# Decode attention plus MLP on one core: inner loops with computed addresses, w2 in 13 rows, and the selects moved to the end of a unit

## The chip, the cores and the metric

The kernel runs on one core of one Trainium2 chip. Time is what the device needs for one execution, in microseconds (us): the median of several runs. A profiled execution of its own gives the rows that are quoted; its clock starts with the span. The engines are TensorE (PE, with its weight loads as PEld), VectorE (DVE), ScalarE (ACT), GpSimd (POOL) and SyncE (SP), which here issues nearly all DMAs into one queue.

## The reference, cut to what matters

```python
x = A_x                                  # (8, 1, 640), bf16
xn = _layernorm(x)
return x + A(xn, k_cache, v_cache, wq, wo) + B(xn, w1, b1, w2, b2)

# A: decode attention, B=8, 32 heads, 4096 keys, Dh=128, one query each
q = (x @ wq).reshape(B, 1, 32, 128).transpose(0, 2, 1, 3)
scores = einsum("bhqd,bhkd->bhqk", q, k_cache) * 128 ** -0.5
o = einsum("bhqk,bhkd->bhqd", softmax(scores), v_cache)
return o.transpose(0, 2, 1, 3).reshape(B, 1, 4096) @ wo

# B: y = layernorm(x); gelu(y @ w1 + b1) @ w2 + b2, F = 1728
```

The two caches are 268 MB each and are read once. Everything else is about 15 MB.

## The kernel before, in words

The work is cut into 32 **units**. Unit i is one batch row and one group of 8 heads: K(i) and V(i), 8.39 MB each, every one loaded by a single DMA of 128 descriptors of 64 KB. A partition holds 256 keys of one head (16 partitions to a head). K(i) goes to slot KA or KB by turns, V(i) to the one slot VS. SyncE's queue holds the order K0, K1, V0, K2, V1, K3, V2 and so on; `load_k(i)` waits until slot i-2 is free, `load_v(i)` until the product P times V of unit i-1 is done (`pv`), and what stands behind a waiting load waits too.

Scores of a unit are made in two ways at once. For 176 of the 256 keys of a partition, VectorE multiplies K by the broadcast query and sums over Dh (`dve_chunk`: a product, a sum of the two halves, a reduction), in three chunks of 58, 59 and 59 keys. For the other 80 keys TensorE transposes K (`pe_T`, ten tiles of 8 keys), ScalarE copies each tile from PSUM (`act_T`, an eviction), and TensorE multiplies it by the query (`pe_QK`). That yields 8 candidates for each key, of which a mask picks one: the **selects** (`dve_sel`, a product and a reduction in PSUM, twice 40 keys), between the second chunk and the third. `dve_max` finds the maximum and makes the bias of the softmax; `act_exp` runs eight exponentials on ScalarE; `pe_RS` sums them; `pe_PV` multiplies by V in 256 matmuls; `act_O`, `dve_rinv` and `o_norm` scale the result.

The query's broadcast for VectorE is a matmul (`pe_qbc`) and an eviction (`act_qbc`); before, both run ahead of K's arrival. A tiny memset on GpSimd (`k_ready`) waits for K(i), and TensorE waits for that memset.

The order of each engine is written by hand: every step has a position (`at(o + 52, dve_sel, i, 0)`), the steps are recorded in that order for each engine, and then replayed into instruction streams. Part of the units is recorded as loops: on VectorE and ScalarE 15 turns of two units after two unrolled units, on TensorE a loop over all units after the first. In a TensorE turn stand the broadcast and scores of unit r, then row sum and P times V of unit r-1. On ScalarE the exponentials of unit i stand after the evictions of unit i+1 for i = 0 alone; later ones stand ahead of them (position 90):

```python
at(o + 52, dve_sel, i, 0)
at(o + 55, dve_sel, i, 1)
at(o + 58, dve_chunk, i, 2)
at(o + 84, dve_max, i)
at(o + 90 if i else o + Q + 45, act_exp, i)
at(o + Q + 48, pe_RS, i)
at(o + Q + 57, dve_rinv, i)
at(o + Q + 50, pe_PV, i)
```

Ahead of the units: layer norms, q = xn @ wq (160 matmuls, after wq has landed), and the MLP. Its first layer needs w1's columns spread out, by ten copies on VectorE and ScalarE (`spread_w1`); its second layer has w2 in 128 half rows of 13.5 rows each, with zeros beside them and 136 matmuls (`pe_mlp2`). K1 and V0 wait for q's last matmul (`qw`), since their slots hold weights until then. Behind the units: wo, in part through selection matmuls and folds (`pe_sel`, `dve_fold`, `fin_wl`, `fin_wn`), and the store.

Of the kernel before, what the change touches and what calls it, by code (L numbers as in the profile page):

```python
# [14 lines left out]
P = 128  # L15
# [12 lines left out]
class _Eng:  # L28
# [17 lines left out]
    def sig(self, inst):  # L46
        self.n += 1
        inst.call[3] = (self.sem, 1)
        return (self.sem, self.n)

# [17 lines left out]
class _Slot:  # L68


    def __init__(self, slots, i, lo, n):
        self.slots, self.i, self.lo, self.n = slots, i, lo, n

    def at(self, i):
        return self.slots[:, i % 2, self.lo:self.lo + self.n]
# [29 lines left out]
def _emit(e, call, wait=None, turn=None):  # L105
    name, a, k, inc = call
    a = [x.at(x.i if turn is None else turn) if isinstance(x, _Slot) else x for x in a]
    if name == "wait_ge":
        e.wait_ge(a[0], a[1] if wait is None else wait, **k)
        return  # L110
    inst = getattr(e, name)(*a, **k)  # L111
    if inc is not None:
        inst.then_inc(*inc)


def _replay(e, calls):
    for call in calls:
        _emit(e, call)


def _same(x):
    if isinstance(x, _Slot):
        return ("slot", x.lo, x.n)
    if hasattr(x, "ap") and hasattr(x, "offset"):
        return (x.tensor.name, x.offset, str(x.ap), str(x.dtype))
    return str(x)


def _steps(turns):

    body = turns[0]
    assert len({len(t) for t in turns}) == 1, [len(t) for t in turns]
    grow = []
    for j, (name, args, kw, inc) in enumerate(body):
        step = 0
        for r in range(1, len(turns)):
            name_r, args_r, kw_r, inc_r = turns[r][j]
            assert name_r == name and inc_r == inc and sorted(kw_r) == sorted(kw), (j, name, name_r)
            if name == "wait_ge":
                assert args_r[0] is args[0]  # L140
                if r == 1:
                    step = args_r[1] - args[1]
                assert args_r[1] == args[1] + r * step and args[1] > 0 and step >= 0, (j, args, args_r)
            else:
                assert [_same(x) for x in args_r] == [_same(x) for x in args], (j, name)
                assert [_same(kw_r[x]) for x in sorted(kw)] == [_same(kw[x]) for x in sorted(kw)], (j, name)
        grow.append(step)
    return grow


def _replay_loop(e, calls, a, b, n):

    size = (b - a) // n
    assert size * n == b - a and n >= 2
    _replay(e, calls[:a])
    grow = _steps([calls[a + r * size:a + (r + 1) * size] for r in range(n)])
    with e.bass.Fori(0, n, engines=OrderedEngineSet([e.engine])) as r:
        for call, step in zip(calls[a:a + size], grow):
            _emit(e, call, call[1][1] + r * step if step else None)
    _replay(e, calls[b:])  # L160


def _replay_pe(e, calls, head, mid, end, late):
# [4 lines left out]
    g1, g2 = _steps(first[:-1]), _steps([[c for c in t if not _late(c, late)] for t in second])  # L168
    _replay(e, calls[:head[0]])
    with e.bass.Fori(1, n + 1, engines=OrderedEngineSet([e.engine])) as r:  # L170
        reg = e.to_reg(r)
        with e.If_lt(reg, n):
            for call, step in zip(first[0], g1):
                _emit(e, call, call[1][1] + (r - 1) * step if step else None, r)
        g = iter(g2)
        for call in second[0]:
            if _late(call, late):
                e.wait_ge(call[1][0], (r >> (n.bit_length() - 1)) * 16 + 1)
            else:
                step = next(g)  # L180
                _emit(e, call, call[1][1] + (r - 1) * step if step else None)
        with e.If_eq(reg, n - 1):
            _replay(e, first[-1])
    assert n & (n - 1) == 0
    _replay(e, calls[end:])


def _late(call, late):
    return call[0] == "wait_ge" and any(call[1][0] is x for x in late)


def bass_parallel_sum__gqa_block_cached__mixer_channel_mlp__decode_kernel(
# [23 lines left out]
    FQ = F // (P // 2)  # L216
    FH = FQ // 2
    PAD = D // 10
    SCALE = float(DH) ** -0.5
    TPB = 8  # L220
    NS = 2
    LOOP0, LOOPN = 2, 15
# [6 lines left out]
    assert FQ * (P // 2) == F and FQ == 2 * FH + 1  # L229

    def jp_of(i):
        return 80

    def chunks(i):
        jd = NKEY - jp_of(i)
        n = 3
        return [(jd * c // n, jd * (c + 1) // n) for c in range(n)]
# [3 lines left out]

    group0 = [0]
    for i_ in range(NQ):
        group0.append(group0[-1] + jp_of(i_) // TPB)
# [4 lines left out]
    with ExitStack() as es:  # L249
# [4 lines left out]
        S_sb = sb("S_sb", [P, 3, SLOT], BF)  # L254
        tile = [S_sb[:, s, :].rearrange("p (j d) -> p j d", d=DH) for s in range(3)]
# [16 lines left out]

        w2_sb = scratch(F * D // P + 2 * PAD)
        b1_sb = scratch(F, 1).rearrange("p (c f) -> p c f", c=1)
        b1r_sb = scratch((FH + 1) * P, 1).rearrange("p (c j m) -> p c j m", c=1, m=P)
        w1r_sb = scratch(DC * (FH + 1) * P).rearrange("p (c j m) -> p c j m", c=DC, m=P)
# [6 lines left out]
        hT_sb = scratch((FH + 1) * B).rearrange("p (c b) -> p c b", b=B)  # L283
        hh_sb = scratch(2 * (FH + 1) * B).rearrange("p (w c b) -> p w c b", w=2, b=B)
        par_sb = scratch(4).bitcast(F32)
        iota_i = scratch(2 * P).bitcast(I32)
        iota_h = scratch(2 * HS).bitcast(I32)
        mtmp = scratch(2 * 2 * HS).bitcast(F32).rearrange("p (w n) -> p w n", w=2)
        ones_sb = scratch(B, 1)
        zeros_sb = scratch(P)  # L290
        assert o_[0] <= SLOT

        KT_sb = sb("KT_sb", [P, NS, TPB, P], BF)
        Sd_sb = sb("Sd_sb", [P, 2, NKEY], F32)
# [6 lines left out]
        oU_sb = sb("oU_sb", [P, 2, HS], F32)  # L301
# [3 lines left out]
        mx_sb = sb("mx_sb", [P, 32], F32)  # L305
        mxT_sb = sb("mxT_sb", [P, 32], F32)
        mq_sb = sb("mq_sb", [P, 2], F32)
        mb_sb = sb("mb_sb", [P, 32], F32)
        mbT_sb = sb("mbT_sb", [P, 32], F32)
        NB_sb = sb("NB_sb", [P, 2, HS], F32)  # L310
# [3 lines left out]
        kr_sb = sb("kr_sb", [P, 1], F32)  # L314
# [8 lines left out]
        ACC_ps = ps("ACC_ps", [P, 512], F32)  # L323
        TRB, SBK = [_Bank(), _Bank()], [_Bank(), _Bank()]
        PVB, QBB, CHB, ACCB = _Bank(), _Bank(), _Bank(), _Bank()
        QT_ps = CH_ps[:, 0:H * B]
        HT_ps = CH_ps[:, H * B:H * B + (FH + 1) * B]
        RS_ps = CH_ps[:, 384:384 + HS]
        OUT_ps = QB_ps[:, :].bitcast(BF)
        assert H * B + (FH + 1) * B <= 384  # L330
# [21 lines left out]

        def load_k(i):
            s = kslot(i)
            if i >= 2:
                sp.wait(tk[("kt", i - 2)], tk[("km", i - 2)])
            elif s == KB:
                sp.wait(tk["qw"])
            tk[("k", i)] = ld_s[s].sig(sp.dma_start(tile[s], cache_src(A_k_cache, i)))

# [13 lines left out]
        def load_wl(q):  # L374
            sp.wait(tk[("kt", NQ - 2)], tk[("km", NQ - 2)])
# [12 lines left out]
        def consts_pool():  # L388
            pool.iota(iota_h, [[-HP, HS]], base=0, channel_multiplier=1)
            tk["iota"] = pool.sig(pool.iota(iota_i, [[1, P]], base=0, channel_multiplier=-1))  # L390
            for d, (ap, v) in zip([None] * (6 - len(ld_vl)) + ld_vl, (
                    (zeros_sb, 0.0), (w2_sb[:, 0:PAD], 0.0), (w2_sb[:, PAD + F * D // P:], 0.0), (ones_sb, 1.0),
                    (mx_sb[:, :], 0.0), (mb_sb[:, :], 0.0))):
# [487 lines left out]
```

## Time and profile before

| | |
|---|---|
| Median of 3 runs | 1283.71 us (1283.64 to 1284.03) |
| Profiled execution | 1283.58 us, its span 1282.3 us |
| Bytes read | 551.80 MB, 430 GB/s over the span |
| Busy: PE, DVE, ACT, POOL | 667.4 (52%), 1099.9 (86%), 483.8 (38%), 98.6 us (8%) |
| Mean granted TensorE clock | 0.592 |

A row of the chain has start, length, and what ran or what was waited for. A row of the timeline has start, length, engine, operation, output and inputs, a count, and in brackets how long the engine had been idle and what ended that. SPq and ACTq are issues of DMAs. All helper lines are L111, so groups are told by their tiles.

### The profile page before, as it was taken

The page shows a single profiled execution, that of the slowest core. Times are in us where ns is not written, and L with a number is a line of the kernel's source. Part 1 is how long each engine was busy: PE and PEld are TensorE (multiplying, and loading weights), DVE is VectorE, ACT ScalarE, POOL GpSimd, SP SyncE. Part 2 cuts the span into 40 slices and gives each one's busy share as a digit, 9 for nine tenths or more (in the row PEclk, how much of TensorE's full clock was granted, in tenths as well). Part 3 has the DMA queues.
Part 4 walks back from the last instruction along what each step waited for, and adds up shares of the span by engine and source line. Part 5 has one row for each costly group of instructions (what it writes and reads, how often), then busy time and mean ns, then how long its engine had stood idle before and what let it go on. Part 6 is the DMA issues. An engine that isn't in the chain of part 4 may idle for free.

```text
span 1282.3 us, 34538 instructions
## 1 busy us (share of the span) xinstructions
PE 667.4 (52%) x13994; PEld 569.3 (44%) x13994; DVE 1099.9 (86%) x677; ACT 483.8 (38%) x908; POOL 98.6 (8%) x112
## 2 busy tenths in 40 slices
PE   4463555564544664544654544654545655545645
PEld 3352444453443553433553534543434544434545
DVE  3599998988888988888988888988889988889885
ACT  3343333344432344423344423344323444323441
POOL 1011110000000000000000000000000000000001
PEclk9955565565656666556666556665556655556655
DMA  9999999999999999999999999999999999999998
GB/s 401 449 421 434 433 431 431 438 433 431 431 440 431 431 431 440 431 429 433 442 429 429 433 442 429 431 431 442 431 430 431 444 427 433 429 444 427 433 419 358
DMA packets 11509, 552.00 MB, mean 430 GB/s; under 512 B 1245, under 2 KB 2278, under 8 KB 2279
## 3 DMA queue, kind: packets, MB, share of 16 engines
q1 hardware_dynamic: 11424, 551.79, 99.6%
q8 instruction: 9, 0.15, 0.0%
q10 hardware_dynamic: 70, 0.03, 0.0%
q14 instruction: 6, 0.04, 0.0%
HBM read 551.80 MB, written 0.01 MB: 430 GB/s over the span
## 4 chain that ended last, share of the span: by engine, by line
DMA 74%; PE 17%; DVE 7%; issue 1%; ACT 0%; SPq 0%; DVEq 0%; ACTq 0%
DMA S_sb<-in_A_v_cache_dram 69%; PE PV_ps L111 16%; DVE S_sb L111 4%; DMA S_sb<-in_A_k_cache_dram 3%; DVE Sd_sb L111 2%; DMA S_sb<-in_A_wo_dram 2%; PE TR_ps L111 1%; ACT P_sb L111 0%; PE S_ps L111 0%; DVE S_ps L111 0%; SPq L111 0%; ACT KT_sb L111 0%; DVE mx_sb L111 0%; PE ACC_ps L111 0%; DVE mxT_sb L111 0%
## 5 line engine op out<-in xcount | busy, mean ns | idle before, releaser
L111 PE MATMUL TR_ps<-ident_bf,S_sb 128*128 128x128 bf16 (+1 forms) x2570 | 340.6, 270 | 363.5 <-POOL kr_sb L111 344.8
L111 DVE TENSOR_TENSOR S_sb<-S_sb,qbc_sb 128x7552 bf16<-128x7552 bf16 (+1 forms) x96 | 388.7, 4049 | 124.7 <-DMA S_sb<-in_A_k_cache_dram 124.3
L111 PEld LDWEIGHTS TR_ps<-ident_bf,S_sb 128*128 (+2 forms) x2570 | 243.4, 102 | 423.7 <-issue 351.6
L111 DVE TENSOR_REDUCE Sd_sb<-S_sb 128x59 f32<-128x3776 bf16 (+1 forms) x96 | 390.2, 4064 | 6.0
L111 ACT ACTIVATE KT_sb<-TR_ps 128x1024 bf16<-128x1024 bf16 x320 | 327.1, 1024 | 116.6 <-PE TR_ps L111 106.8
L111 PE MATMUL PV_ps<-P_sb,S_sb 128*128 128x8 bf16 x8192 | 224.3, 175 | 144.5 <-DMA S_sb<-in_A_v_cache_dram 140.5
L111 PEld LDWEIGHTS PV_ps<-P_sb,S_sb 128*128 128x128 bf16 x8192 | 221.3, 103 | 147.4 <-DMA S_sb<-in_A_v_cache_dram 143.2
L111 ACT ACTIVATE P_sb<-Sd_sb,NB_sb 128x256 bf16<-128x256 f32 x256 | 126.3, 494 | 229.0 <-DVE NB_sb L111 229.0
L111 DVE TENSOR_TENSOR S_sb<-S_sb 128x3776 bf16<-128x3776 bf16 (+1 forms) x96 | 202.9, 2114 | 3.3
L111 ACT ACTIVATE oU_sb<-PV_ps 128x8 f32<-128x8 f32 x31 | 5.5, 178 | 384.3 <-PE PV_ps L111 384.3
L111 PE MATMUL S_ps<-qrep_sb,KT_sb 128*128 128x8 bf16 x2560 | 121.3, 177 | 51.7 <-ACT KT_sb L111 48.5
L111 PEld LDWEIGHTS S_ps<-qrep_sb,KT_sb 128*128 128x128 bf16 x2560 | 90.7, 101 | 82.1 <-ACT KT_sb L111 35.9
L111 POOL TENSOR_TENSOR oT_sb<-oU_sb,ri_sb 128x8 bf16<-128x8 f32 x31 | 69.3, 2235 | 383.5 <-DVE S_sb L111 341.8
L111 POOL COPY qrep_sb<-qT_sb 128x128 bf16<-128x128 bf16 x32 | 19.7, 615 | 477.6 <-PE S_ps L111 451.4
L111 ACT ACTIVATION_READ_ACCUMULATOR P_sb<-Sd_sb,NB_sb 128x1 f32 x256 | 47.8, 187 | 0.0
L111 DVE TENSOR_REDUCE Sd_sb<-S_ps 128x40 f32<-128x320 f32 x64 | 31.4, 491 | 2.2
L111 DVE TENSOR_TENSOR S_ps<-S_ps,mask_sb 128x320 f32<-128x320 f32 (+1 forms) x66 | 32.7, 495 | 0.0
L111 POOL MEMSET kr_sb<- 128x1 f32 x32 | 3.1, 98 | 293.4 <-DMA S_sb<-in_A_k_cache_dram 293.4
L111 ACT ACTIVATE qbc_sb<-QB_ps 128x128 bf16<-128x128 f32 x32 | 8.9, 278 | 41.8 <-PE QB_ps L111 41.8
L111 PE MATMUL QB_ps<-ident_bf,qrep_sb 128*128 128x128 bf16 x32 | 9.1, 284 | 26.1 <-DVE S_sb L111 15.0
L111 PE MATMUL CH_ps<-rs_sb,ones_f 128*128 128x8 f32 x64 | 15.4, 313 | 4.6 <-ACT P_sb L111 4.2
L111 PEld LDWEIGHTS QB_ps<-ident_bf,qrep_sb 128*128 128x128 bf16 x32 | 3.3, 104 | 29.0 <-ACT oU_sb L111 21.0
(58 smaller groups left out, 142.4 us busy)
## 6 DMA issues: line engine op xcount, KB each, us to landing
S_sb<-in_A_wq_dram SPq DMA_DIRECT2D x1, 5120.0 KB, 25.4
S_sb<-in_B_w_dram SPq DMA_DIRECT2D x2, 2160.0 KB, 11.1
S_sb<-in_A_v_cache_dram SPq DMA_DIRECT2D x1, 4096.0 KB, 15.3
S_sb<-in_A_v_cache_dram SPq DMA_DIRECT2D x1, 2816.0 KB, 18.6
S_sb<-in_A_wo_dram SPq DMA_DIRECT2D x1, 2560.0 KB, 31.2
S_sb<-in_A_wo_dram SPq DMA_DIRECT2D x1, 1280.0 KB, 33.9
S_sb<-in_A_v_cache_dram SPq DMA_DIRECT2D x1, 1280.0 KB, 21.4
S_sb<-in_A_wo_dram SPq DMA_DIRECT2D x1, 640.0 KB, 22.6
```

What stands on the lines that cost most here:

```text
L111: inst = getattr(e, name)(*a, **k)
```

## The change

1. **VectorE's chunks** become one of 176 keys. The two selects move behind it (positions 80 and 82), with 64 and 16 keys. The score, bias and unscaled output buffers are single instead of double, so the reduction of unit i waits for the exponentials of unit i-1.
2. **K's arrival** is waited for by the broadcast matmul `pe_qbc`, ahead of transposes and of VectorE's product; GpSimd's marker goes. `pe_qbc` also waits for both PSUM banks of scores, that is for the selects of the unit before. `act_qbc` of unit i+1 stays ahead of the exponentials of unit i on ScalarE.
3. **K's slot** is free with the last select (`s`), where it was with the last reduction and transpose.
4. **Inner loops**: ScalarE's ten evictions are five turns of two, with computed waits; TensorE's scores of unit 0 and 13 columns of the first layer are loops with computed addresses. Loops over units start earlier (VectorE at unit 0, ScalarE at unit 2, one unit a turn).
5. **MLP**: w1 is read with a stride instead of being spread; the last 64 columns are doubled on GpSimd. w2 comes as 13 rows to a partition and 64 single rows to every other partition, over zeros; 70 matmuls instead of 136. The 64 rows and b2 are issued on SyncE, behind a wait for the memset of the zeros.
6. The exponential that loaded ScalarE's table early (`act_O(-1)`) is a copy; two layer norm steps are merged; two folds at the end are one.

```diff
         def load_k(i):
             s = kslot(i)
             if i >= 2:
-                sp.wait(tk[("kt", i - 2)], tk[("km", i - 2)])
+                sp.wait(tk[("s", i - 2)])
...
+        def load_w2():
+            tk["w2"] = [ld_w2.sig(sp.dma_start(
+                w2_sb[:, 0:FR * D], B_w2[0:FR * P].rearrange("(p r) n -> p (r n)", r=FR)))]
+            sp.wait((ld_s[KB].sem, 1))
+            tk["w2"] = [ld_w2.sig(sp.dma_start(w2_sb[0:P:2, FR * D:], B_w2[FR * P:]))]
...
         def pe_qbc(i):
-            pe.wait(tk[("qrep", i)], tk["id"])
+            pe.wait(tk[("qrep", i)], *tk[("kk", i)])
             QBB.use(pe)
+            for b_ in SBK:
+                b_.use(pe)
...
+        def scores(i):
+            n = jp_of(i) // TPB
+            last = None
+            for u in range(n // 2):
+                act.calls.append(["_in", (u,), {}, None])
+                if i == 0:
+                    pe.calls.append(["_in", (u,), {}, None])
+                for t in (2 * u, 2 * u + 1):
+                    pe_T(i, t)
+                    act_T(i, t)
+                    if i == 0 and t % 2:
+                        pe_QK(i, t - 1)
+                        pe_QK(i, t)
+                    elif i and t:
+                        pe_QK(i, t - 1)
...
         def dve_chunk(i, c):
-            dve.wait(tk[("k", i)], tk[("qb", i)])
+            dve.wait(tk[("qb", i)])
...
-            dve.wait(t, tk.get(("exp", i - 2)))
+            dve.wait(t, tk[("exp", i - 1)])
...
         def act_O(i):
             PVB.use(act)
+            act.wait(tk.get(("on", i - 1)), tk[("ri", i)])
...
-            at(o - 2, k_ready, i)
             at(o - 11, pe_qbc, i)
             at(o - 10.5, act_qbc, i)
...
+            at(o, scores, i)
             at(o + 2, dve_chunk, i, 0)
-            at(o + 26, dve_chunk, i, 1)
-            at(o + 52, dve_sel, i, 0)
-            at(o + 55, dve_sel, i, 1)
-            at(o + 58, dve_chunk, i, 2)
+            at(o + 80, dve_sel, i, 0)
+            at(o + 82, dve_sel, i, 1)
             at(o + 84, dve_max, i)
             at(o + 90 if i else o + Q + 45, act_exp, i)
```

523 lines of the change are left out of this document (284 added, 239 removed).

## The prediction

> **What bounds the kernel now.** I read the page first (span, the 40 slices, the shares of the chain), then the chain of waits in order of time, and then the timeline of each engine for the first 145 us. K(i), V(i) are the two 8.39 MB loads of unit i.
>
> ```profile
> span 1282.3 us, 34538 instructions
> DMA  9999999999999999999999999999999999999998
> GB/s 401 449 421 434 433 431 431 438 433 431 431 440 431 431 431 440 431 429 433 442 429 429 433 442 429 431 431 442 431 430 431 444 427 433 429 444 427 433 419 358
> q8 instruction: 9, 0.15, 0.0%
> DMA 74%; PE 17%; DVE 7%; issue 1%; ACT 0%; SPq 0%; DVEq 0%; ACTq 0%
> 434.87 7.01 PE PV_ps L111 x256
> 441.90 31.63 DMA S_sb<-in_A_v_cache_dram
> 473.57 7.01 PE PV_ps L111 x256
> 1279.33 0.72 PE ACC_ps L111 x20
> ```
>
> The transfers never stop: every slice but the last is 90% busy or more. The chain alternates 31.6 us of a V load and 7.0 us of P times V, 38.70 us per unit (434.87 to 473.57), that is 19.35 us per load. PE's 17% costs nothing: while it runs, the next K load flows. So only three things can move the time: bytes, the two ends, or a moment in which the single load queue has nothing left. In steady state it is well filled:
>
> ```profile
> 415.60 4.02 DVE L111 TENSOR_TENSOR S_sb<-S_sb,qbc_sb 128x7424 bf16<-128x7424 bf16 x1 [4.29 <-DMA S_sb<-in_A_k_cache_dram]
> 449.81 0.23 DVE L111 TENSOR_SCALAR NB_sb<-off_sb,mbT_sb 128x8 f32<-128x8 f32 x1
> 454.29 4.02 DVE L111 TENSOR_TENSOR S_sb<-S_sb,qbc_sb 128x7424 bf16<-128x7424 bf16 x1 [4.26 <-DMA S_sb<-in_A_k_cache_dram]
> ```
>
> A K load has landed at 454.29; V is issued at 441.90, 12.4 us before it would be missed, and DVE has 4.3 us to spare in each unit. The start is tighter, because DVE works off a backlog there:
>
> ```profile
> 79.08 0.33 SPq L111 DMA_DIRECT2D S_sb<-in_A_k_cache_dram  x1
> 96.64 0.33 SPq L111 DMA_DIRECT2D S_sb<-in_A_v_cache_dram  x1
> 46.33 0.10 POOL L111 MEMSET kr_sb<- 128x1 f32 x1 [9.41 <-DMA S_sb<-in_A_k_cache_dram]
> 144.58 0.10 POOL L111 MEMSET kr_sb<- 128x1 f32 x1 [3.03 <-DMA S_sb<-in_A_k_cache_dram]
> 0.74 0.39 SPq L111
> 9.57 8.39 ACT L111 ACTIVATE S_sb<-S_sb 128x896 bf16<-128x896 bf16 x5 [2.59 <-DMA S_sb<-in_B_w_dram]
> 1280.96 0.30 ACTq L111 DMA_DIRECT2D out_dram<-out_sb  x1
> ```
>
> K(0) landed at 46.3 and K(3) at 144.55 (GpSimd's memsets wait for them). The order is K0 K1 V0 K2 V1 K3, so V(1) landed near 144.55 - 19.35 = 125.2. How late may V(1) be issued? A load into an empty queue costs its bytes plus an overhead: w1 was issued first, at 0.74, and landed at 9.57 for 2.21 MB, 5.1 us at the steady 433 GB/s (8.39 MB in 19.35 us): 3.7 us over. That was a cold start. I take 2.5 us, midway between this and the 1.3 us from the output's issue (10 KB, 1280.96) to the end of the span. V(1) is then late from 125.2 - 19.35 - 2.5 = **103.35** on; before, it was issued at 96.64, 6.7 us early.
>
> **The change part by part: unit 0 and 1.** V(1) waits for PV(0), PV(0) for exp(0), and ScalarE has exp(0) behind all evictions of unit 1, in both kernels. Before, the transposes of unit 1 began when K(1) landed, 66.40, and were done when exp(0)'s bias came. Now the query's broadcast matmul of unit 1 waits for both selects of unit 0 (it uses the banks' tickets), the transposes of unit 1 stand behind it on TensorE, and the selects are the last work of unit 0 on VectorE. So evictions, exp(0) and PV(0) follow VectorE instead of running beside it. Durations:
>
> ```profile
> 36.97 0.29 PE L111 MATMUL QB_ps<-ident_bf,qrep_sb 128*128 128x128 bf16 x1 [0.87 <-POOL qrep_sb L111]
> 37.29 0.28 ACT L111 ACTIVATE qbc_sb<-QB_ps 128x128 bf16<-128x128 f32 x1 [14.13 <-PE QB_ps L111]
> 46.30 4.02 DVE L111 TENSOR_TENSOR S_sb<-S_sb,qbc_sb 128x7424 bf16<-128x7424 bf16 x1 [9.74 <-DMA S_sb<-in_A_k_cache_dram]
> 50.36 2.09 DVE L111 TENSOR_TENSOR S_sb<-S_sb 128x3712 bf16<-128x3712 bf16 x1
> 66.70 0.49 DVE L111 TENSOR_TENSOR S_ps<-S_ps,mask_sb 128x320 f32<-128x320 f32 x1
> 68.56 0.16 DVE L111 COPY ri_sb<-off_sb 128x8 f32<-128x8 f32 x1
> 68.63 4.08 DVE L111 TENSOR_TENSOR S_sb<-S_sb,qbc_sb 128x7552 bf16<-128x7552 bf16 x1
> 79.03 0.42 DVE L111 TENSOR_REDUCE mx_sb<-Sd_sb 128x1 f32<-128x256 f32 x1
> 80.41 0.23 DVE L111 TENSOR_SCALAR NB_sb<-off_sb,mbT_sb 128x8 f32<-128x8 f32 x1
> 114.66 0.05 DVE NB_sb L111
> 114.95 4.04 DVE S_sb L111
> 66.40 2.31 PE L111 MATMUL TR_ps<-ident_bf,S_sb 128*128 128x128 bf16 x16 [5.38 <-POOL kr_sb L111]
> 79.16 1.02 ACT L111 ACTIVATE KT_sb<-TR_ps 128x1024 bf16<-128x1024 bf16 x1 [0.36 <-PE TR_ps L111]
> 58.80 1.28 ACT L111 ACT_TABLE_LOAD   x1
> 80.67 0.51 ACT L111 ACTIVATE P_sb<-Sd_sb,NB_sb 128x256 bf16<-128x256 f32 x1 [0.49 <-DVE NB_sb L111]
> 84.53 0.19 ACT L111 ACTIVATION_READ_ACCUMULATOR P_sb<-Sd_sb,NB_sb 128x1 f32 x1
> 85.42 5.80 PE L111 MATMUL PV_ps<-P_sb,S_sb 128*128 128x8 bf16 x211
> 95.23 1.37 PE L111 MATMUL PV_ps<-P_sb,S_sb 128*128 128x8 bf16 x45 [4.02 <-issue]
> ```
>
> 1. The broadcast now waits for K(0): matmul to eviction 0.32, eviction 0.28, and 0.1 for two hand-overs: VectorE starts at 47.0 instead of 46.30.
> 2. Nine products, sums and reductions become three. They took 20.40 (46.30 to 66.70) plus 10.40 (68.63 to 79.03) = 30.80 us. A product of 7424 takes 4.02, a sum of half as many 2.09: a fixed part of 0.16 in each. Six are saved, 0.96: 29.85 us (bounds: nothing saved, 30.8). The reciprocal's 0.1 and the selects' 1.86 (66.70 to 68.56; now 64 and 16 keys instead of 40 and 40, the same elements) follow: the selects end at 78.9. K(2) goes out at 79.0, as before (79.08); V(0) had landed by 85.42, so that is in time.
> 3. Transposes of unit 1 start at 79.1. From the first transpose to the end of the last eviction it took 66.40 to 80.18 = 13.78. Bounds: the evictions' own 10 x 1.02 plus 1.24 for the first two tiles, 11.5; and 13.78 plus a turn of ScalarE's new loop five times, at most 1.2 us (VectorE's own turn, 114.71 to 114.95, is 0.24 long). I take 13.9, near the measured pace: 93.0.
> 4. The table load for Exp, 1.28, stood before unit 1's evictions; now it is right ahead of exp(0): 94.3.
> 5. Eight exponentials and the row sum until the first PV: 80.67 to 85.42, 4.75: PV(0) starts at 99.05.
> 6. PV(0) took 7.0 of work (the chain's 7.01) and 4.02 of a stall in which TensorE waited for instructions. The same stall stands after 127 matmuls here:
>
> ```profile
> 27.45 0.67 PE L111 MATMUL ACC_ps<-S_sb 128*128 128x8 bf16 x19 [0.49 <-issue]
> 34.57 1.53 PE L111 MATMUL CH_ps<-S_sb 128*128 128x8 bf16 x52 [3.58 <-issue]
> ```
>
> Between 27.45 and 30.99 it ran 19 + 108 matmuls, then waited. With a weight load each, that is 254 instructions; q8's 0.15 MB in 9 packets is 16.7 KB each, so a packet holds about 256, and the next one comes about 7.1 us after its predecessor is entered (27.45 to 34.57). In the changed program PV(0) begins after 1081 TensorE instructions, where it was 1562; with the same spacing packets end after 67 and 195 of PV(0)'s matmuls. The second is asked for at 100.9 and needed at 104.4; by the row it comes at 108.4, a stall of 4.0. But K(2), which lands at 125.2 - 19.35 = 105.85, has its bytes through near 105, and the packet then has nothing to queue behind: 0 and 4.0 are the bounds, I take 2.2. PV(0) ends at 99.05 + 7.0 + 2.2 = 108.25, and V(1) is issued at **108.3**.
>
> [...]
>
> So V(1) is 108.3 - 103.35 = **4.95 us** late, the queue is empty for that long, and with transfers busy throughout nothing later gives it back. Next points: VectorE starts unit 1 at 80.5, behind unit 0's maximum (1.6 us, 79.03 to 80.64); exp(1) follows unit 1's maximum at 80.5 + 29.85 + 2.0 + 1.6 = 113.9, PV(1) ends at about 137.5, V(2) then goes out 9 us before its own limit; steady state follows.
>
> **The other edits, at nothing.** The first layer's spreading copies (8.39 us on ScalarE) go, TensorE starts earlier and has 70 instead of 136 matmuls in the second layer: all of that ends before wq lands (25.4 us to landing by the page) and K(0) at 46.3 covers it; cover ends only if q's last matmul, before 36.1, came after 43.8. w2 has the same bytes; its 64 rows of 1280 bytes and the bias on SyncE wait for a memset that runs while w1's 5.1 us flow: -0.1 to +0.2. Some 700 instructions fewer, at 16.7 KB per 256, are 46 KB: 0.1 us gained. GpSimd's K marker goes; nobody else waited for it. The single score buffer makes unit i+1's reduction wait for exp(i): 98.35 against 98.4, and then hidden in steady state, where exp(i) ends about 5 us after K(i+1) lands. ScalarE's copy of PV waits for the reciprocal, about 31 us after K lands: its next job needs the next K anyway, at 38.7. In the tail the selects move behind the last reduction but stay ahead of the maximum, behind which the folds stand in both kernels:
>
> ```profile
> 1262.53 0.23 DVE L111 TENSOR_SCALAR NB_sb<-off_sb,mbT_sb 128x8 f32<-128x8 f32 x1
> ```
>
> The last matmuls wait for wo (1279.33), 17 us after it: 0, at most +1.
>
> **Rivals.** (a) No stall in PV(0): the packet is there. V(1) at 106.1, 2.75 late: 1286.3. For it: a shorter program; against: 4.02 and 3.58. (b) *The other side*: evictions at ScalarE's own pace (11.5 us, so 2.4 less) and no stall: V(1) at 103.7, 0.3 late, and on time if the overhead is under 2.1: 1283.6, no change. It decides at 103.35. That the hold on the selects does not bite in unit 1 gives the same time. (c) Steady state breaks: exp(i) now stands behind the broadcast of unit i+1, so PV(i) can begin only 0.8 + 4.0 (80.67 to 84.72) + 13.9 + 0.7 = 19.4 us after K(i+1), just where V(i) lands (19.35); PV ends at 26.5, and V(i+1) must be out by 36.2. From 9.7 us more on, each of some 29 units pays the rest: 1 us over gives 1313. Nothing in the rows is that long. (d) Each backward jump of ScalarE's five-turn loop costs a fetch of 4.02: 20 us per unit, 10.3 over the limit of (c), in 29 units 300 us: 1583. Against: 30 units ran through loops before with 9 packets of code on q8. [...] (e) Faster: the first slice's 401 against 431 GB/s is 2.2 us of start, and the tail 3 us; no edit reaches the first issue or the last, so it would take all of the one and 0.9 of the other: 1280.5.
>
> **How the numbers follow.** The profiled execution took 1283.58, the median of the runs is 1283.71, 0.01% apart. 1283.58 + 4.95 = **1288.5**. Chances: forecast 0.66, (a) 0.12, (b) 0.12, (c) and (d) 0.05, (e) 0.05. Own bounds of the forecast: stall 0 to 4.0 (-2.2, +1.8), evictions (-2.4, +1.1), overhead 1.3 to 3.7 (-1.2, +1.2), chunk (+0.95): below no gap at all, 1283.6, up to 1293.5; all high ends together are unlikely. The range runs from 1283.3, so that (b) is inside, to 1292.0. A measurement here tells 0.2% (2.57 us) from no change. Slower by more: 0.62 of the forecast, half of (a), (c), (d): 0.73. Within: the rest of the forecast 0.04, half of (a), (b): 0.22. Faster: 0.05.
>
> **What would show it.** Right: the transposes of unit 1 start near 79 and not when K(1) lands; exp(0) near 94, a table load ahead of it; PV(0) from 99 to 106-110; V(1)'s issue after 103.4; a hole in GB/s between about 105 and 110, and none later; K(3) landing near 149.5; each unit still 38.70. Wrong: V(1) issued before 103.4; evictions at 1.02 each; the packet already there; a unit longer than 38.70; or a different tail after the last wo landing.

## The result and the profile after

The changed kernel takes **1289.01 us** (median of 6 runs, 1288.82 to 1289.47) against 1283.75 us (6 runs, 1283.64 to 1284.03) for the kernel before: ratio 1.0042, 95% interval 1.0029 to 1.0054. The profiled execution took 1288.82 us, its span 1287.0. The forecast was 1288.5, in a range of 1283.3 to 1292.0.

The page of the changed kernel, the lines that stood for before in the prediction:

```profile
span 1287.0 us, 34448 instructions
DMA  9998999999999999999999999999999999999998
GB/s 403 447 425 363 428 424 450 426 428 450 426 428 442 434 428 428 446 428 426 448 428 428 440 436 428 430 444 428 426 448 428 428 444 432 428 434 442 426 420 364
q8 instruction: 7, 0.11, 0.0%
DMA 76%; PE 18%; issue 2%; DVE 2%; ACT 1%; SPq 0%; POOL 0%; ACTq 0%; DVEq 0%; POOLq 0%
```

One slice of 40 has changed its digit: the fourth, 96.5 to 128.7 us, fell from 434 to 363 GB/s. 71 GB/s over 32.2 us are 2.3 MB, 5.3 us of loading at the mean rate. Everything else looks as it did, so the place of the loss is known from the page alone. The same place in steps of 1 us (stretch and its length, then busy time and instructions of PE, PEld, DVE, ACT and POOL, PE's granted clock, the DMA share, GB/s):

```profile
101.00:102.00 1.00, 1.00 (x44) 1.00 (x41) 1.00 (x1) 0.00 (x0) 0.00 (x0) 1.00 0.76 328
102.00:103.00 1.00, 1.00 (x44) 1.00 (x42) 1.00 (x1) 0.00 (x0) 0.00 (x0) 1.00 0.08 16
103.00:104.00 1.00, 1.00 (x44) 1.00 (x41) 1.00 (x1) 0.00 (x0) 0.00 (x0) 1.00 0.00 0
106.00:107.00 1.00, 0.84 (x32) 0.74 (x28) 1.00 (x1) 0.00 (x0) 0.00 (x0) 1.00 0.08 16
107.00:108.00 1.00, 0.00 (x0) 0.00 (x0) 1.00 (x1) 0.00 (x0) 0.00 (x0) 1.00 1.79 590
```

The view books a packet's bytes in the step in which the packet begins, so that a share can pass 1, as in the last row. From about 102.0 to 107.8, then, no packet of a load begins. (16 GB/s in a row are one instruction fetch of 16,384 bytes.) By the DMA packets in the trace the 16 DMA engines end K(2) between 102.16 and 104.14, on average at 102.88, and begin V(1) between 107.83 and 108.78, on average at 108.07. So an engine has no load for 5.2 us on average, while TensorE works through P times V of unit 0. The loads' issues in the timeline of SP:

```profile
79.53 0.33 SPq L218 DMA_DIRECT2D S_sb<-in_A_k_cache_dram  x1
106.87 0.33 SPq L218 DMA_DIRECT2D S_sb<-in_A_v_cache_dram  x1
```

The second row is V(1), issued at 96.64 before. The hole ends 0.96 us after this issue, when V(1)'s first packet begins (107.83). The chain from there on, the starts of PV(3) and PV(4), then PV(3) in the timeline of the kernel before:

```profile
207.22 7.04 PE PV_ps L218 x256
245.92 7.03 PE PV_ps L218 x256
```

```profile
202.62 6.99 PE L111 MATMUL PV_ps<-P_sb,S_sb 128*128 128x8 bf16 x256 [2.11 <-DMA S_sb<-in_A_v_cache_dram]
```

PV(3) starts 4.60 us later (207.22 - 202.62), a unit still takes 38.70, and from PV(3) to the end of the span it is 1079.7 us before and 1079.8 after. So the whole of the span's 4.7 us has been lost by 207 us. The other 0.5 us lies outside the span: the profiled executions are 1.28 us longer than their span before and 1.82 after.

The steps of the prediction, from the timelines of PE, of ACT and of DVE of the changed kernel:

```profile
46.96 0.27 PE L218 MATMUL QB_ps<-ident_bf,qrep_sb 128*128 128x128 bf16 x1 [4.59 <-DMA S_sb<-in_A_k_cache_dram]
79.56 0.29 PE L218 MATMUL QB_ps<-ident_bf,qrep_sb 128*128 128x128 bf16 x1 [8.19 <-DVE ini_sb L218]
79.73 2.23 PE L218 MATMUL TR_ps<-ident_bf,S_sb 128*128 128x128 bf16 x16
99.78 7.06 PE L218 MATMUL PV_ps<-P_sb,S_sb 128*128 128x8 bf16 x256
```

```profile
91.67 2.17 ACT L218 ACTIVATE KT_sb<-TR_ps 128x1024 bf16<-128x1024 bf16 x2 [1.04 <-PE TR_ps L218]
93.86 1.28 ACT L218 ACT_TABLE_LOAD   x1
95.15 0.51 ACT L218 ACTIVATE P_sb<-ini_sb 128x256 bf16<-128x256 f32 x1
```

```profile
47.57 11.89 DVE L218 TENSOR_TENSOR S_sb<-S_sb,qbc_sb 128x22528 bf16<-128x22528 bf16 x1 [5.86 <-ACT qbc_sb L218]
65.65 11.89 DVE L218 TENSOR_REDUCE ini_sb<-S_sb 128x176 f32<-128x11264 bf16 x1
79.21 0.29 DVE L218 TENSOR_REDUCE ini_sb<-S_ps 128x16 f32<-128x128 f32 x1
```

TensorE idles 8.19 us and is released by VectorE's last select (ending 79.50); only then come the broadcast and the transposes of unit 1, which started at 66.40 before. The evictions, the table load, exp(0) and PV(0) follow in one line, and PV(0) runs its 256 matmuls without a stop.

### The profile page after: what moved, and what is told of

Its sections match the earlier page's. It is cut to its first block, busy times and chain, and to the rows that moved or that the text cites. A ratio compares the mean times of both kernels' runs of the same rounds, so it can differ in the third digit from the quotient of the medians.

```text
span 1287.0 us, 34448 instructions
## 1 busy us (share of the span) xinstructions
PE 679.6 (53%) x13931; PEld 581.9 (45%) x13931; DVE 1070.0 (83%) x471; ACT 466.3 (36%) x903; POOL 76.7 (6%) x78
## 4 chain that ended last, share of the span: by engine, by line
DMA 76%; PE 18%; issue 2%; DVE 2%; ACT 1%; SPq 0%; POOL 0%; ACTq 0%; DVEq 0%; POOLq 0%
DMA S_sb<-in_A_v_cache_dram 71%; PE PV_ps L218 16%; DMA S_sb<-in_A_k_cache_dram 3%; DMA S_sb<-in_A_wo_dram 2%; DVE S_sb L218 1%; PE TR_ps L218 1%; ACT P_sb L218 1%; PE S_ps L218 0%; ACT KT_sb L218 0%; SPq L218 0%; DVE S_ps L218 0%; DVE ini_sb L218 0%; ACT L218 0%; PE QB_ps L218 0%; POOL S_sb L218 0%
## 5 line engine op out<-in xcount | busy, mean ns | idle before, releaser
L218 DVE TENSOR_TENSOR S_sb<-S_sb,qbc_sb 128x22528 bf16<-128x22528 bf16 x32 | 380.5, 11892 | 151.4 <-ACT qbc_sb L218 151.1
L218 DVE TENSOR_REDUCE ini_sb<-S_sb 128x176 f32<-128x11264 bf16 x32 | 380.4, 11886 | 4.1 <-ACT P_sb L218 0.2
L218 PEld LDWEIGHTS TR_ps<-ident_bf,S_sb 128*128 (+1 forms) x2570 | 245.0, 102 | 66.6 <-DVE S_sb L218 7.5
L218 DVE TENSOR_TENSOR S_sb<-S_sb 128x11264 bf16<-128x11264 bf16 x32 | 192.8, 6025 | 1.1
L218 ACT ACTIVATE P_sb<-ini_sb 128x256 bf16<-128x256 f32 x256 | 126.1, 496 | 4.2 <-DVE ini_sb L218 4.2
L218 POOL COPY qrep_sb<-qT_sb 128x128 bf16<-128x128 bf16 x32 | 64.9, 2028 | 775.7 <-PE S_ps L218 744.1
L218 ACT ACTIVATION_READ_ACCUMULATOR P_sb<-ini_sb 128x1 f32 x256 | 48.5, 190 | 0.0
L218 DVE TENSOR_REDUCE ini_sb<-S_ps 128x64 f32<-128x512 f32 x64 | 31.5, 492 | 2.2
L218 DVE TENSOR_TENSOR S_ps<-S_ps,mask_sb 128x512 f32<-128x512 f32 (+1 forms) x65 | 32.1, 493 | 0.1
L218 POOL TENSOR_TENSOR oT_sb<-oU_sb,ri_sb 128x8 bf16<-128x8 f32 x31 | 7.1, 229 | 406.5 <-ACT oU_sb L218 406.5
```

The source lines that it names most:

```text
L218: inst = getattr(e, name)(*out, **kw)
```

## The experiments

**Theory 1**: V(1) goes out when PV(0) ends, PV(0) follows the chain selects, transposes, evictions, exp(0), and every microsecond that V(1) is late after about 102 is lost for good. **Rivals**: the time is lost elsewhere (the longer first stage, the single buffers, the units themselves), or another wait takes over when the chain is made shorter. Twelve kernels ran, each beside the kernel before. The columns: start of PV(0); length and end of a stop within it; issue of V(1) (of its first half in the five kernels that cut it); start of PV(3); median of the runs and ratio to the kernel before with its interval.

| kernel | PV(0) | stop, until | V(1) out | PV(3) | us | ratio |
|---|---|---|---|---|---|---|
| before | 85.42 | 4.02, 95.23 | 96.64 | 202.62 | 1283.75 | |
| changed | 99.78 | none | 106.87 | 207.22 | 1289.01 | 1.0042 (1.0029 to 1.0054) |
| a_table | 98.63 | 1.04, 105.02 | 106.82 | 207.15 | 1288.62 | 1.0040 (1.0026 to 1.0053) |
| a_hold | 96.28 | 3.13, 104.75 | 106.56 | 206.87 | 1288.63 | 1.0040 (1.0026 to 1.0054) |
| a_slope | 103.22 | none | 110.22 | 210.43 | 1291.24 | 1.0060 (1.0046 to 1.0074) |
| a_early | 96.27 | 3.21, 104.84 | 106.64 | 207.12 | 1288.80 | 1.0037 (1.0023 to 1.0050) |
| p_bad | 94.98 | 4.05, 102.59 | 106.24 | 206.95 | 1288.59 | 1.0039 (1.0026 to 1.0053) |
| p_good | 95.95 | 3.21, 102.39 | 106.51 | 206.99 | 1288.71 | 1.0040 (1.0027 to 1.0054) |
| a_half | 96.24 | 3.49, 105.08 | 99.83 | 201.72 | 1284.99 | 1.0011 (1.0002 to 1.0020) |
| o_half | 99.01 | 0.65, 105.01 | 102.60 | 203.55 | 1286.85 | 1.0026 (1.0016 to 1.0036) |
| a_one | 96.19 | 3.44, 104.98 | 99.78 | 201.50 | 1282.73 | 0.9995 (0.9986 to 1.0004) |
| o_one | 100.13 | none | 103.73 | 204.13 | 1284.93 | 1.0008 (0.9998 to 1.0017) |
| a_one_b2 | 95.01 | 2.31, 102.67 | 98.60 | 201.48 | 1282.98 | 0.9995 (0.9986 to 1.0004) |
| b_sel | 94.15 | 2.56, 102.49 | 103.89 | 204.43 | 1285.48 | 1.0016 (1.0007 to 1.0025) |

### The slope: a_slope

Three tiny activations that switch ScalarE's table stand ahead of exp(0); their results go nowhere. ScalarE's timeline has three table loads of 1.28 us there, where the changed kernel has one.

```diff
+        def act_more():
+            for k, f in enumerate((ACT.Gelu_apprx_tanh, ACT.Exp, ACT.Gelu_apprx_tanh)):
+                act.activation(more_sb[:, k, :], off_sb[:, :], f)
+        at(Q + 44.5, act_more)
```

> The changed kernel with two more table loads and three tiny exponentials or gelus of a constant (their results unused) on ScalarE right ahead of exp(0): 2 x 1.28 + 3 x 0.2 = 3.2 us. Theory: V(1) at 110.1, time 1289.0 + 3.2 = 1292.2, since the queue is empty already and no slack is left. Rival (V(1)'s issue does not bound): 1289.0.

Measured: 1291.24 us. PE's timeline of a_slope, then SP's:

```profile
103.22 6.98 PE L218 MATMUL PV_ps<-P_sb,S_sb 128*128 128x8 bf16 x256
```

```profile
110.22 0.33 SPq L218 DMA_DIRECT2D S_sb<-in_A_v_cache_dram  x1
```

V(1) moved by 3.35 us and PV(3) by 3.21 (210.43 against 207.22). What delays exp(0) delays the whole run, as theory 1 has it: the profiled execution by 3.27 us (1288.82 to 1292.09). But this is the fastest of the changed kernel's runs against the slowest of a_slope's; the medians are 2.23 us apart, two thirds of the 3.2 that were expected. Why the medians gain less than V(1) was late is not shown.

### A shorter chain: a_table, a_hold, a_early

a_table loads the table early again (an exponential on a constant in `act_O(-1)`, as in the kernel before). a_hold lets the broadcast and the transposes go ahead of unit 0's selects, and holds only the first score matmul of each bank. a_early has both, and the broadcast ahead of K's arrival as well.

```diff
 # a_table
+            if i < 0:
+                tk[("oU", i)] = PVB.used(act, act.sig(act.activation(oU_sb[:, :], off_sb[:, :], ACT.Exp)))
+                return
 # a_hold, in pe_qbc
-            for b_ in SBK:
-                b_.use(pe)
 # a_hold, in pe_QK
             pe.wait(tk[("ev", i, t)])
+            if t in HALF[:2]:
+                SBK[HALF.index(t)].use(pe)
 # a_early: K is waited for in scores() and dve_chunk(), not in pe_qbc
-            pe.wait(tk[("qrep", i)], *tk[("kk", i)])
+            pe.wait(tk[("qrep", i)])
...
+            pe.wait(*tk[("kk", i)])
...
-            dve.wait(tk[("qb", i)])
+            dve.wait(tk[("k", i)], tk[("qb", i)])
```

> The changed kernel with one undo: the first copy of PV on ScalarE is an exponential of a constant again, so that the table load for Exp stands ahead of unit 1's evictions. Theory (V(1) is issued late, and each us counts in full): exp(0) starts 1.29 us earlier, V(1) goes out at 105.6 instead of 106.87, time 1289.0 - 1.3 = 1287.7. Rival (the 5 us come from the start of the program: q's last matmul 5 us later, K(0) landing 0.4 later, a cold restart of the queue): no change, 1289.0.

> The changed kernel with the wait for the selects moved from the query's broadcast to the first score matmul of each PSUM bank. Theory: the first two transposes and evictions of unit 1 run when K(1) lands, the first scores follow the selects at 79.6 instead of 82.06; V(1) at about 104.5, time 1286.7 (1286.2 to 1287.2). Rival (start of the program): 1289.0.

> The changed kernel with three undos: the early table load, the wait for the selects at the first score matmul, and the query's broadcast ahead of K's arrival (VectorE and the first transpose wait for K themselves). Selects stay last, inner loops and w2 stay as changed. Theory: 1.3 + 2.4 + 0.8 us earlier, V(1) at 102.4, within 0.2 of where the queue runs empty: 1284.4 (1284.0 to 1285.0), of which 0.4 is K(0)'s later landing. Rival (start of the program, or the selects' place by itself): 1287 or more.

Measured: 1288.62, 1288.63 and 1288.80 us, all as slow as the changed kernel; all three expectations of theory 1 failed. (One of a_early's five runs took 1286.15; no trace shows why.) PV(0) did start earlier, by 1.15, 3.50 and 3.51 us. PE's timeline of a_early, then one of its 1 us steps:

```profile
96.27 5.35 PE L218 MATMUL PV_ps<-P_sb,S_sb 128*128 128x8 bf16 x195
104.84 1.78 PE L218 MATMUL PV_ps<-P_sb,S_sb 128*128 128x8 bf16 x61 [3.21 <-issue]
```

```profile
103.00:104.00 1.00, 0.00 (x0) 0.00 (x0) 1.00 (x1) 0.00 (x0) 0.00 (x0) 1.00 0.00 0
```

After 195 matmuls TensorE stands for 3.21 us and waits for nothing that the profile shows ("issue"). The prediction had put a packet's end after 195 matmuls of PV(0). In all three kernels the next packet is there at 104.75 to 105.02, whenever PV(0) began, so V(1) stays at 106.6 to 106.8. Theory 1 falls in part: there are **two bounds at almost the same time**, the chain (the changed kernel needs the packet at about 105.1 and just finds it: its fetch ended at 103.67, and at its stops at 39.86 and 90.19, and at those of the kernel before at 34.57 and 95.23, TensorE went on 1.3 to 1.5 us after the end of a fetch) and the packet. A shorter chain turns into a wait for instructions.

### Moving the end of the packet: p_bad and p_good

Both are a_early with matmuls added ahead of unit 0, into columns of PSUM that nobody reads: 68 put packet ends after 0 and 127 matmuls of PV(0), 80 after 115 and 243.

```diff
+            for k in range(68):    # 80 in p_good
+                pe.matmul(PV_ps[:, HS + 4 * k:HS + 4 * k + 4], ident_bf[:, :], ident_bf[:, 0:4], start=True, stop=True)
             CHB.use(pe)
```

> The kernel of a_early (V(1) at 106.64, PV(0) held 3.21 us after 195 matmuls by a missing instruction packet) with 68 tiny extra matmuls ahead of unit 0, which move the packets' ends in PV(0) from after 67 and 195 matmuls to after 0 and 127. New theory (in a_early, a_hold and a_table V(1)'s issue is set by the packet, which comes at about 104.8, when K(2)'s bytes are through, whatever the softmax chain does): PV(0) stops after 127 matmuls at 99.8, goes on at 103.5 to 104.8 and has 3.5 us left: V(1) at 107.0 to 108.8, time 1289.2 to 1291.0 against 1288.8. Rival (another bound): 1288.8.

> The same with 80 extra matmuls instead of 68: packets end after 115 and 243 matmuls of PV(0), and the first of the two is asked for before TensorE waits for the exponentials. New theory: no stop at 115, a stop at 243 until about 104.8, 13 matmuls left: V(1) at 105.2, time 1287.4 against a_early's 1288.8. Rival (another bound): 1288.8; if extra instructions cost by themselves, more than that.

PE's timeline of p_bad, then of p_good:

```profile
94.98 3.56 PE L218 MATMUL PV_ps<-P_sb,S_sb 128*128 128x8 bf16 x128
102.59 3.62 PE L218 MATMUL PV_ps<-P_sb,S_sb 128*128 128x8 bf16 x128 [4.05 <-issue]
```

```profile
95.95 3.24 PE L218 MATMUL PV_ps<-P_sb,S_sb 128*128 128x8 bf16 x116
102.39 4.08 PE L218 MATMUL PV_ps<-P_sb,S_sb 128*128 128x8 bf16 x140 [3.21 <-issue]
```

The stop comes after 128 and 116 matmuls, where the added instructions put it (within one): it is the end of a packet, and not something in PV(0). But V(1) moved by 0.4 and 0.1 us only, and the times, 1288.59 and 1288.71, are those of a_early. The price that was expected for a stop further forward, and the gain, did not come: the packet's arrival moved as well, from 104.84 to 102.59 and 102.39. The traces show that the fetch moved, for they hold the fetches themselves (queue q8, one packet of 16,384 bytes each). The 1 us step in which the stop's fetch begins, in a_early, p_bad and p_good:

```profile
102.00:103.00 1.00, 0.00 (x0) 0.00 (x0) 1.00 (x1) 0.00 (x0) 0.00 (x0) 1.00 0.09 25
99.00:100.00 1.00, 0.00 (x0) 0.00 (x0) 1.00 (x1) 0.00 (x0) 0.00 (x0) 1.00 1.28 541
100.00:101.00 1.00, 0.00 (x0) 0.00 (x0) 1.00 (x1) 0.00 (x0) 0.00 (x0) 0.50 0.82 344
```

(25 GB/s are taken as 16,384 bytes and 8,192 more, 541 are 16,384 beside 8 packets of a load of 65,536 bytes, 344 beside 5.) In the traces of the kernel before and of the changed kernel all 13 fetches on q8 that begin ahead of 102.7 do so within 0.01 us of the end of a load's packet; such a packet takes 2.42 us. So in these two a fetch began where a packet of the loads ended; how many packets go ahead of it is left open.

### V(1) without the whole wait: a_half, o_half

If the loss is only that V(1) waits for the end of PV(0), the wait can be cut instead of the chain. a_half (on a_early) and o_half (on the changed kernel) load each V in two DMAs of half the keys. The first waits for the first 128 matmuls of the unit before, the second for all.

```diff
-            sp.wait(tk["qw"] if i == 0 else tk[("pv" if i < NQ - 1 else "pvh", i - 1)])
+            sp.wait(tk["qw"] if i == 0 else tk[("pvh", i - 1)])
...
+                for lo, hi in ((0, 128), (128, 256)):
+                    if lo and i:
+                        sp.wait(tk[("pv", i - 1)])
+                    tk[("v", i)] = [ld_s[VS].sig(sp.dma_start(
+                        tile[VS][:, lo:hi, :], cache_src(A_v_cache, i)[:, lo:hi, :]))]
```

> The kernel of a_early with every V load as two DMAs of half the keys: the first waits for the first 128 matmuls of the unit before, the second for all. Theory: the first half of V(1) goes out at 99.8, before the queue runs empty at about 102, and the second at 106.6 finds 9.7 us of work ahead of it: no hole, 1284.6 (1284.2 to 1285.2), of which 0.4 is K(0)'s later landing and 0.5 lies outside the span. Rival (the start of the program costs the 5 us): 1288.8.

> The changed kernel as it is, with the two DMAs for each V load alone. Theory: the first half of V(1) goes out after 128 matmuls, at 99.78 + 3.5 = 103.3, 1.1 us after the limit: a hole of about 1 us instead of 5, 1285.6 (1285.0 to 1286.3). Rival (start of the program): 1289.0.

Measured: 1284.99 and 1286.85 us. The issue in a_half, then its chain:

```profile
99.83 7.38 SPq L218 DMA_DIRECT2D S_sb<-in_A_v_cache_dram  x2
```

```profile
201.72 7.01 PE PV_ps L218 x256
240.50 7.01 PE PV_ps L218 x256
279.27 7.01 PE PV_ps L218 x256
```

With the first half out at 99.83 no microsecond is empty any more, though PV(0) still stands for 3.49 us. PV(3) starts at 201.72, 5.4 us earlier than in a_early. But a unit now takes 38.77 (240.50 to 279.27) instead of 38.70: over some 30 units that gives 2.1 us back. No expectation had counted these 2.1 us: o_half missed its own range (1285.0 to 1286.3) by 0.55 us, and a_half met its range only because the filled hole brought more than had been expected.

### One cut alone: a_one, o_one

Only V(1) is cut; all other V loads are single again.

```diff
-            sp.wait(tk["qw"] if i == 0 else tk[("pv" if i < NQ - 1 else "pvh", i - 1)])
+            sp.wait(tk["qw"] if i == 0 else tk[("pv" if 1 < i < NQ - 1 else "pvh", i - 1)])
+            if i == 1:
+                tk[("v", i)] = [ld_s[VS].sig(sp.dma_start(
+                    tile[VS][:, 0:128, :], cache_src(A_v_cache, i)[:, 0:128, :]))]
+                sp.wait(tk[("pv", 0)])
+                ld_vl[0].sig(sp.dma_start(tile[VS][:, 128:, :], cache_src(A_v_cache, i)[:, 128:, :]))
+                return
```

> a_early (table load early, hold on the selects only at the first scores, broadcast ahead of K's arrival) with V(1) alone, of all V loads, in two DMAs of half the keys; the first waits for the first 128 matmuls of PV(0), the second for all. Theory (the only loss is that the queue runs empty around 102-107 because V(1) waits for the whole of PV(0); halving every V cost 0.07 us a unit): the first half goes out near 99.8, no slice is empty, PV units are 38.70 again, and the time is that of the two-DMA kernel, 1284.99, less 30 x 0.07: 1282.9. Rival 1 (the changed start itself costs some 1.3 us, K(0) landing 0.4 later among it, so the loss is not only the hole): 1284.2 or more. Rival 2 (two DMAs in the queue for one V cost a time of their own at the seam, not a rate): 1284.99 or more.

> The changed kernel as it is, V(1) alone in two DMAs of half the keys, the first behind the first 128 matmuls of PV(0). Theory: the first half goes out at 102.6, 0.4 us after the point where the queue runs dry; units are 38.70 again; 1286.85 less 2.1 = 1284.75, that is 4.3 under the changed kernel by one DMA's wait alone. Rival (the hole is set by when PV(0) ends, or the change loses time elsewhere too): 1286.5 to 1289.

Measured: **1282.73** (1282.48 to 1284.09, 11 runs) and **1284.93** us (1283.89 to 1285.34, 11 runs). In a_one the issue, two of the steps that were empty, and the chain:

```profile
99.78 7.35 SPq L218 DMA_DIRECT2D S_sb<-in_A_v_cache_dram  x2
```

```profile
102.00:103.00 1.00, 0.00 (x0) 0.00 (x0) 1.00 (x1) 0.00 (x0) 0.00 (x0) 0.50 0.84 320
105.00:106.00 1.00, 1.00 (x38) 1.00 (x39) 1.00 (x1) 0.00 (x0) 0.00 (x0) 0.50 0.83 360
```

```profile
240.20 7.01 PE PV_ps L218 x256
278.90 7.01 PE PV_ps L218 x256
```

320 and 360 GB/s where there was nothing, and 38.70 us a unit. From a_early to a_one only this load has changed (cut in two, the first half with a shorter wait), and 6.07 us of the median are gone (1288.80 to 1282.73; 0.5 of them outside the span). o_one does the same to the changed kernel as it stands, and takes 4.08 of its 5.26 us away, 0.5 of them outside the span as well. Its hole is shorter by more than half: no packet of a load begins in the two steps from 102 to 104, where in the changed kernel it was so from 102.0 to 107.8. The steps in o_one (its profiled execution, 1285.34, is the slowest of its 11 runs):

```profile
102.00:103.00 1.00, 1.00 (x44) 1.00 (x42) 1.00 (x1) 0.00 (x0) 0.00 (x0) 1.00 0.09 16
103.00:104.00 1.00, 1.00 (x44) 1.00 (x41) 1.00 (x1) 0.00 (x0) 0.00 (x0) 1.00 0.00 0
104.00:105.00 1.00, 1.00 (x43) 1.00 (x41) 1.00 (x1) 0.00 (x0) 0.00 (x0) 1.00 1.52 426
```

So the hole is the loss within the span. Whether a_one beats the kernel before can't be told: 0.9995, 0.9986 to 1.0004.

### The first stage: a_one_b2

a_one with b2's load back on ScalarE's own queue, ahead of everything, as before the change.

```diff
-        at(-879, load, "b2", ld_b2, b2_sb, B_b2.rearrange("(o f) -> o f", o=1))
+        at(-897, load, "b2", ld_b2, b2_sb, B_b2.rearrange("(o f) -> o f", o=1), act)
```

> As the kernel with V(1) in two DMAs, and b2's load back on ScalarE's own queue ahead of w1's wait, as in the kernel before. Theory (the five later microseconds of q's last matmul are covered by K(0)'s transfer): the second layer and q end 4 to 5 us earlier, the time moves by 0 to -0.4 (the 0.4 being K(0)'s later landing): 1282.5 to 1282.9. Rival (the longer first stage costs time, as K1 and V0 wait for q's last matmul): 1 us less or more.

The changed kernel's first stage in PE's timeline, then q's last matmuls in a_one_b2:

```profile
13.81 0.19 PE L218 MATMUL ACC_ps<-S_sb 128*128 128x40 bf16 x1 [5.66 <-DMA S_sb<-in_B_b_dram]
15.70 0.87 PE L218 MATMUL CH_ps<-S_sb 128*128 128x8 bf16 x6 [0.48 <-issue]
39.86 1.39 PE L218 MATMUL CH_ps<-S_sb 128*128 128x8 bf16 x46 [3.52 <-issue]
```

```profile
34.60 1.39 PE L218 MATMUL CH_ps<-S_sb 128*128 128x8 bf16 x46 [2.61 <-issue]
```

TensorE waited 5.66 us for b2, which now follows on SyncE; with b2 early, q ends 5.26 us earlier (34.60 against 39.86). The time is 1282.98, just above the 1282.5 to 1282.9 that were expected and no better than a_one's 1282.73. The median span is 0.2 us shorter (1281.2 against 1281.4), and what lies outside the span 0.5 longer. Five microseconds of the first stage were covered by K(0)'s transfer.

### Selects last alone: b_sel

The kernel before, with nothing but the selects moved behind the third chunk.

```diff
-            at(o + 52, dve_sel, i, 0)
-            at(o + 55, dve_sel, i, 1)
             at(o + 58, dve_chunk, i, 2)
+            at(o + 80, dve_sel, i, 0)
+            at(o + 82, dve_sel, i, 1)
```

> The kernel before with one edit: the two selects stand behind the third chunk instead of behind the second; chunks, loops, w2 and buffers are as before. Theory (selects last is the edit that costs: scores of unit 1 wait on TensorE for unit 0's banks, evictions behind them, exp(0) and PV(0) late): the first scores of unit 1 come at 79 instead of near 69, V(1) goes out at 103.7 to 106.5 instead of 96.6 against a limit of 101.8 to 102.2, and the time is 1285.5 to 1288, about 1286.7; a unit stays 38.70. Rival (the hole needs the other parts of the change, single buffers, the broadcast's hold, or the inner loops): V(1) before 101 and 1283.6.

Measured: 1285.48 us (1284.82 to 1287.92, 11 runs), at the lower end of what was expected. PE's timeline of b_sel, then SP's, then the chain:

```profile
78.21 0.39 PE L111 MATMUL S_ps<-qrep_sb,KT_sb 128*128 128x8 bf16 x8 [9.69 <-DVE Sd_sb L111]
```

```profile
103.89 0.33 SPq L111 DMA_DIRECT2D S_sb<-in_A_v_cache_dram  x1
```

```profile
204.43 7.01 PE PV_ps L111 x256
```

This one move makes TensorE wait 9.69 us for the select of unit 0, sends V(1) out 7.25 us later (103.89) and costs 1.83 us, with the old chunks, buffers, loops and weights. Of that lateness 5.4 us are the slack that the kernel before had, since PV(3) is only 1.81 us later (204.43 against 202.62). The rest of the change's loss can be followed in a_early, which keeps the selects last and has the transposes and the table load early again. Its V(1) goes out 2.75 us later than b_sel's (106.64 against 103.89), and the packet accounts for that: it is there 2.35 us later (104.84 against 102.49) and leaves 61 matmuls to do instead of 45 (1.78 us against 1.37). In the changed kernel the longer chain (the transposes behind the selects, the table load) and the packet end within 0.3 us of each other, so their shares can't be told apart.

## Why the prediction was right, point by point

- **What bounds the kernel**: right. What moved the time was a moment in which the one load queue had nothing left, and beside it 0.5 us outside the span. a_one and o_one show it: one DMA's wait was changed, and most of the loss was gone.
- **Step 1**, VectorE starts at 47.0: it was 47.57. K(0) landed 0.4 later than before (46.71 against 46.28 in the traces), which no term had, and released TensorE at 46.96; b2's place accounts for 0.2 of that (the first transpose behind K(0) starts at 46.63 in a_one_b2 against 46.85 in a_one).
- **Step 2**, the chunk in 29.85, the selects done at 78.9, K(2) out at 79.0: 29.97 (47.57 to 77.54), 79.50 and 79.53.
- **Step 3**, transposes at 79.1, 13.9 to the last eviction, 93.0: 79.73, 14.1, 93.84. The hold on the selects bites as said; a_hold without it starts PV(0) 3.50 us earlier.
- **Step 4**, the table load ahead of exp(0), 94.3: 1.28, and exp(0) at 95.15.
- **Step 5**, 4.75 to PV(0), 99.05: 4.63 and 99.78.
- **Step 6**, 7.0 and a stall of 2.2, V(1) at 108.3: the size was wrong. No stall; V(1) at 106.87, 1.4 earlier. The lower bound, 0, was what happened: the packet that the row had coming at 108.4 was there by 105.1 (the 196th matmul's place at 27 ns each). (The row's own 7.1 us after 100.9 give 108.0, a stall of 3.6 and not 4.0.) The reason that the prediction gave for the lower bound, that K(2)'s bytes would be through, is what the trace shows, but earlier than forecast: the fetch begins at 102.44, as a last packet of K(2) ends, and K(2) had landed by 104.7 and not at 105.85. So the hole too lies earlier, from 102 to 108 and not from 105 to 110. There was no stop at this matmul here; a_early, with PV(0) begun 3.51 us earlier, stood for 3.21 us at it.
- **The limit of 103.35** was mis-sized the other way. V(1), K(3), V(2), K(4), V(3) are five loads of 19.35 = 96.75, and V(1)'s issue stands 100.35 ahead of PV(3): the restart of the empty queue costs 3.6 us and not 2.5. (V(1) alone took 22.9 us from issue to landing, 3.5 us over 19.35.) w1's row had said 3.7, and I had halved the distance to the other end. Against the kernel before, the limit is thus 106.87 - 4.60 = 102.3.
- **The sum**: 4.95 late was forecast, 4.60 measured. 2.2 too much of stall stood against 0.8 too little ahead of V(1)'s issue (106.87 where steps 1 to 5 and 7.0 of work gave 106.05) and 1.1 too little of restart. That they nearly cancelled is luck; the path and the wait were right. 0.5 us outside the span made up the rest, and no step had it.
- **The other edits at nothing**: right in their effect, wrong in one working. q's last matmul ended at 41.25 and not before 36.1: I had not seen that the first layer's accumulation opens with b2, which was moved behind other issues on SyncE. 41.25 is still under the 43.8 at which the cover ends, and in a_one_b2, where q ends at 35.99, the span is only 0.2 us shorter, less than a_one's runs differ among themselves (1281.1 to 1282.7). The single score buffer was on the edge that the prediction named: the reduction of unit 1 waited 0.22 us for exp(0). Units and tail were unchanged, as said.
- **The rivals**: (a), no stall, had the right stall and gave 1286.3 by the wrong limit. With it came one of the signs that the prediction had named for being wrong, the packet already there. (b), the other side, (c), (d) and (e) did not come: V(1) was late, a unit is 38.70, no gap between ScalarE's evictions of unit 1 is over 1.04 us where (d) had 4.02 at each turn, and the kernel is not faster. What the prediction lacked was that the packet would be a second bound right behind the chain, so that undoing the hold on the selects or the late table load brings nothing by itself.

## What to carry to other kernels

Where one queue of loads sets the time, as here, ask for each load when its issue must come and what its wait is made of. The slack was smaller here in the start-up of the pipeline than in steady state (for V(1) 5.4 us, by b_sel; in steady state 12.4 us, from V's issue at 441.90 to K's landing at 454.29 in the kernel before), and a step that is free there (selects last) emptied the queue once, which nothing gave back: from PV(3) to the end it took 1079.7 us before and 1079.8 after. When two bounds end close together (within 0.3 us here), shortening one may show no gain, as in a_table, a_hold and a_early: cut the wait that both feed, here by letting the first half of a buffer's load go when the first half of the buffer is free. Cut only where it is needed; the same cut in every unit cost 2.26 us (1284.99 in a_half, 1282.73 in a_one).

## What the runs showed of the hardware

- **The restart of the empty queue cost 3.5 to 4.0 us** beyond the bytes: from V(1)'s issue to PV(3) it took 100.2 to 100.7 us in all eight kernels with a hole and an uncut V(1) (106.87 to 207.22, 110.22 to 210.43, 103.89 to 204.43), where five loads are 96.75. In the changed kernel 0.96 us of it pass until the first packet begins, and the first packets take up to 3.53 us instead of 2.42; the rest was not looked into.
- **Stops at the end of an instruction packet.** By the prediction's estimate of about 256 instructions to a packet (two stops 127 matmuls apart in the kernel before, with a weight load each), packets end after 195 matmuls of PV(0), or after 127 and 115 with 68 and 80 matmuls added; TensorE stopped after 195, 128 and 116, and after 211 in the kernel before and in b_sel, for 0.65 to 4.05 us. With 128 matmuls at 27 ns (3.5 us) from the end of one packet to the end of the next, and the first end placed by that count, the next packet came 4.2 us (o_half) to 7.6 us (p_bad) after the first end. A fetch on q8 takes 0.9 to 1.3 us in the traces of the kernel before and of the changed kernel. In the kernels on the changed one that stopped, TensorE went on at 104.75 to 105.08 where the first end lay between 98 and 101 us, and at 102.39 to 102.67 where it lay by 97; the fetch began between 102 and 103 in a_early, a_half, o_half and a_one, and between 99 and 101 in p_bad, p_good and a_one_b2. In a_slope, which came to the first end at 105.0 (67 matmuls after 103.22), TensorE did not stop. What sets a fetch's begin stays open.
- **Two DMAs for one V** (32 KB descriptors instead of 64 KB) cost 0.07 us per load of 8.39 MB (a unit of 38.77 us in a_half, 38.70 in a_one).
- **A turn of the inner loop over the first layer's columns cost TensorE 0.37 to 0.48 us** of "issue" (13 turns, changed kernel). Between ScalarE's evictions of unit 1 in the same kernel every gap that its timeline shows (0.16 to 1.04 us) is put down to TensorE, none to "issue".
- **The time outside the span was 1.3 or 1.8 us**, the same within about 0.1 in all runs of a kernel. It was 1.3 in the kernel before, b_sel, a_half, o_half, a_one and o_one, and 1.8 in the changed kernel, a_table, a_hold, a_slope, a_early, p_bad, p_good and a_one_b2, which differs from a_one by one DMA's queue. The cause was not found.
- **a_one starts PV(3) 1.1 us earlier than the kernel before** (201.50 against 202.62), though its first transpose of K(0) starts 0.4 later (46.85 against 46.48). The first work on K(3) places the difference: TensorE, released by the load, starts on it at 143.60 in a_one; before, GpSimd's memset for it came at 144.58 and the load had landed at 144.53. Before, V(1) landed at 125.19, 20.5 us after K(2) (104.66) instead of 19.35. What held it up there was not looked into.
